# A spectral filter with a mixture of experts: batch 0's last routing, the splitting of expert weights and batch 1's crossing product are rearranged

## The chip, the cores and the metric

The kernel runs on one core of a Trainium2 chip. The metric is device microseconds of one execution. An execution of the kernel before takes 1332.23 us (median of three runs, 1332.09 to 1335.22). PE is the matmul engine (TensorE), PEld its weight loads, DVE the vector engine, ACT the scalar engine, POOL the GpSimd engine, and SP the engine that here only issues transfers (DMA).

## The reference, cut to what matters

```python
X = np.fft.rfft(x, axis=1)                       # x: (8, 2496, 256)
y = np.fft.irfft(X * (filt_r + 1j * filt_i)[None], n=2496, axis=1)
x = y.reshape(8 * 2496, 256)
xn = x / (norm(x) + 1e-06); en = emb / (norm(emb) + 1e-06)      # 8 experts
logits = xn @ en.T / tau
expert = argmax(logits); gate = softmax(logits)[expert]
out[rows of e] = gate * (maximum(rows @ w1[e], 0) @ w2[e])      # 256 -> 1024 -> 256
```

All in f32. Every row goes to one expert, so 19,968 rows are sorted by expert on the chip.

## The kernel before, in words

The transform. 2496 = 64 x 39, so the transform of a batch is a product over 39 (`s1`), a product over 64 (`s2`), the filter, a product back over 64 (`sa`, constant `m1`), and a product back over 39 (`sb`, `csb`). Between them data changes its layout: batch 0 does it on the chip (`conv_first`), later batches through DRAM, `SD` after `s1` and `ZD` after `sa`. Real and imaginary parts stand in 64 partitions each. The filter multiplies both by the real part of the filter (`yy`) and the crossed parts by its imaginary part (`xs`); for the crossing, two ACT copies exchange the halves of 64 partitions (L673, L674), and an addition brings `yy` and `xs` together (L681) before `sa`.

The routing. `conv_sb` works through 11 pairs of tiles. For each it makes the rows (f16 high and low part, `rows`), transposes them (`tp`, `yT`) and multiplies with the expert vectors (`lp`). In chunks of 3, 4 and 4 pairs `route` then finds the largest logit, its one-hot (`oh`), the running count by products with triangles (`rk`), the row's position in the sorted buffer `XS` (`ixi`), the exponentials (`ex`) and the gate (`se`, written into each row). Rows are sent by POOL, 128 at a time (`scatter_rows`). In batch 0 the factor `f` of a chunk comes from 12 steps of a root and two products on POOL (L169 to L178, L794, L795).

The experts. A slot is 256 rows of one expert. SP reads them transposed (`xT`), `up` makes `ph` in four parts of 12 products, ACT and DVE make the rectified high and low part (`h`), `down` adds 12 products into `po` two parts later. Weights are held as f16 pairs. `weight_halves` makes them for one expert after the other, one step at each call of `next(prep)`: the largest magnitudes (DVE for `w1`, ACT for `w2`: `wj`), a product with the identity and one with ones to spread the largest over partitions (`pm`, `ps`; `spread_max`), scales (`wsc`), and then four quarters `j` (`halves`): the high part on ACT, the low part on DVE. The first quarter of experts 1 to 7 is scaled and rounded by two ACT passes instead, and its low part is a POOL subtraction (L319 to L321).

What sets the order. Until the routing of batch 0 is done, the order on PE, DVE, ACT and SP is that in which the code is written; two tables, `WLOADS` and `PREPS`, say at which step of `head` an expert's weights are loaded and a step of `weight_halves` is made. After it, slots of batch g and the transform of batch g+1 are mixed: `spread` is called twice for each part of a slot, makes one step of `weight_halves`, every fourth time a load, and as many steps of the next batch as `pace` asks for. A planner of the framework then fixes each engine's queue. Every engine works its queue in order, so an instruction that waits holds all behind it.

Of the kernel before, what the change touches and what calls it, by code (L numbers as in the profile page):

```python
# [53 lines left out]
WLOADS = (0, 13, 17, 19, 26, 28, 36, 38, 44, 48)  # L54
PREPS = (21, 25, 57, 58, 59, 60, 66, 67, 68, 69, 70, 71, 72, 73)
# [4 lines left out]
def moe_spectral_kernel(  # L60
# [8 lines left out]
    m1: bass.AP,  # L69
    csb: bass.AP,  # L70
# [45 lines left out]
    csb_sb = const.tile([120, P], F32, tag="csb", name="csb_sb")  # L116
    sgn_sb = const.tile([P, NK2], F32, tag="sgn", name="sgn_sb")
# [3 lines left out]
    for q, t, a in ((nc.scalar, c1_sb, c1), (nc.scalar, c2_sb, c2), (nc.gpsimd, sgn_sb, sgn), (nc.gpsimd, m1_sb, m1),  # L121
                    (nc.gpsimd, emb_sb, emb), (nc.gpsimd, lt32, lt), (nc.gpsimd, tau_sb, tau),
                    (nc.gpsimd, csb_sb, csb)):
        q.dma_start(t, a)
# [24 lines left out]
    snoi = cst.tile([1, smax], I32, tag="st", name="snoi")  # L149
    nc.gpsimd.iota(snoi, pattern=[[1, smax]], base=0, channel_multiplier=0)  # L150
    sno = const.tile([1, smax], F32, tag="sno", name="sno")
# [69 lines left out]
    wmax = const.tile([P, E, 2], F32, tag="wmax", name="wmax")  # L221
    one32 = const.tile([2, P], F32, tag="one32", name="one32")
    nc.vector.memset(one32, 1.0)
    wtop = const.tile([2, E], F32, tag="wtop", name="wtop")
    wdg = const.tile([2, E, 2], F32, tag="wdg", name="wdg")
# [40 lines left out]
    def weight_halves():  # L266
# [3 lines left out]
        def largest(e, j):  # L270
            pieces = raws[e, j][0] + raws[e, j][1]
            wm = wmx[:, j * 4:j * 4 + len(pieces)]
            for i, r in enumerate(pieces):
                if j:
                    wjunk = cw.tile([P, 1024], F16, tag="hl", bufs=XYB, name=f"wj{e}_{i}")
                    with behind("relu"):
                        nc.scalar.activation(wjunk[:, :r.shape[1]], r, AF.Abs, accum_out=wm[:, i:i + 1])
                else:
                    with behind("lower"):
                        v.tensor_reduce(out=wm[:, i:i + 1], in_=r, axis=AX.X, op=ALU.max, apply_absolute_value=True)  # L280
            v.tensor_reduce(out=wmax[:, e, j:j + 1], in_=wm, axis=AX.X, op=ALU.add if j else ALU.max)

        def spread_max(e, js):

            n = js.stop - js.start
            m = wmax[:, e, js]
            v.tensor_scalar(out=m, in0=m, scalar1=2.0 ** -100, scalar2=None, op0=ALU.max)
            v.tensor_scalar(out=m.bitcast(I32), in0=m.bitcast(I32), scalar1=0x7F800000, scalar2=None,
                            op0=ALU.bitwise_and)
            yield  # L290
# [7 lines left out]
            nc.tensor.matmul(pm[:, :n], one32[:n], wdg[:n, e, :n], start=True, stop=True)  # L298
            v.tensor_scalar(out=wsc[:, e, js].bitcast(I32), in0=pm[:, :n].bitcast(I32), scalar1=0x7F800000,
                            scalar2=None, op0=ALU.bitwise_xor)  # L300

        def scales(e, js):
            for j in range(js.start, js.stop):
                v.tensor_scalar(out=wsc[:, e, j:j + 1], in0=wsc[:, e, j:j + 1], scalar1=2.0 ** (14 if j else 5),
                                scalar2=None, op0=ALU.mult)
            v.reciprocal(winv[:, e, js], wsc[:, e, js])
            if js.stop == 2:
                v.tensor_tensor(out=isc[:, e:e + 1], in0=winv[:, e, 0:1], in1=winv[:, e, 1:2], op=ALU.mult)
# [1043 lines left out]
```

## Time and profile before

| what | us |
|---|---|
| median of the runs | 1332.23 |
| profiled execution | 1332.51 |
| its span, first to last instruction | 1330.7 |
| PE busy | 1252.1 (94%) |
| DVE busy | 889.9 (67%) |
| ACT busy | 745.5 (56%) |
| POOL busy | 550.0 (41%) |
| mean granted TensorE clock, full speed 1 | 0.969 |

A busy share is a mean over stages. The rows below are from single stages: the first expert product begins at 123.29 us, the first product of `y` of batch 1 at 216.36, the first expert product of batch 1 at 303.37. In a row `L106 PE MATMUL ph<-xT,W` is line, engine, operation, and what is written from what; `x24` is a count; what stands in brackets is the idle time of the engine just before, and what ended it.

### The profile page before, as it was taken

The numbers are of one execution on the slowest core, as the hardware profiler recorded it, in microseconds if no ns is written. First come the engines' busy times: TensorE is split into PE (matmuls) and PEld (weight loads), VectorE is DVE, ScalarE is ACT, GpSimd is POOL, SyncE is SP. The second block draws the span as 40 slices with busy tenths as digits, with TensorE's granted clock in tenths as the row PEclk, the third lists the DMA queues.
The fourth block names the chain that finished last, engine by engine and source line by source line (L and its number), as shares of the span: only waits on it lengthen the run. The fifth ranks groups of instructions, "written<-read, shape, count | busy, mean of one in ns | idle before, by whom it ended". The sixth has DMA issues, their size and how long they took to land.

```text
span 1330.7 us, 32603 instructions
## 1 busy us (share of the span) xinstructions
PE 1252.1 (94%) x11240; PEld 1001.9 (75%) x11240; DVE 889.9 (67%) x2853; ACT 745.5 (56%) x1694; POOL 550.0 (41%) x642
## 2 busy tenths in 40 slices
PE   8866889989998999999999999999999999999997
PEld 6533556656677877777787778778878888999997
DVE  3564977875576768858775968597669622466664
ACT  5745577745645665658476747675666233333332
POOL 2363344474354525642654374346423632222222
PEclk9877899979999999999999999999999999999999
DMA  9728856678768775877697678766752422222221
GB/s 327 264 65 247 270 139 172 171 217 229 192 170 209 212 189 153 256 202 185 173 230 213 168 184 240 187 179 183 218 152 58 115 75 49 53 46 49 50 47 37
DMA packets 223223, 218.70 MB, mean 164 GB/s; under 512 B 125006, under 2 KB 168429, under 8 KB 221132
## 3 DMA queue, kind: packets, MB, share of 16 engines
q1 hardware_dynamic: 197226, 158.68, 44.8%
q0 software_dynamic: 25552, 57.72, 14.2%
q8 instruction: 94, 1.54, 0.5%
q14 instruction: 77, 0.63, 0.2%
q10 hardware_dynamic: 274, 0.13, 0.0%
HBM read 116.37 MB, written 79.60 MB: 147 GB/s over the span
## 4 chain that ended last, share of the span: by engine, by line
PE 57%; issue 13%; DVE 8%; DMA 8%; ACT 6%; POOL 5%; SPq 1%; POOLq 0%; ACTq 0%; DVEq 0%
PE ph L1106 20%; PE po L1134 18%; PE s L476 6%; POOL out_dram L1038 3%; PE y L481 3%; PE tp L809 3%; DMA f<-ZD 2%; PE sa L481 2%; DMA a<-SD 2%; PE s L481 2%; PE y L476 1%; DMA f<-in_filt 1%; PE lp L824 1%; PE sa L699 1%; DVE xs L647 1%
## 5 line engine op out<-in xcount | busy, mean ns | idle before, releaser
L1134 PE MATMUL po<-W,h 128*128 128x256 f16 (+1 forms) x3864 | 499.7, 274 | 3.4 <-ACT h L1112 2.1
L1134 PEld LDWEIGHTS <-h 128*128 128x128 f16 x3864 | 367.8, 98 | 89.2 <-issue 45.1
L1106 PE MATMUL ph<-xT,W 128*128 128x256 f16 x3072 | 400.9, 276 | 13.7 <-DVE h L1113 6.4
L1106 PEld LDWEIGHTS <-W 128*128 128x128 f16 x3072 | 295.9, 99 | 93.1 <-issue 45.9
L1112 ACT ACTIVATE h<-ph 128x512 f16<-128x512 f32 (+1 forms) x388 | 203.7, 526 | 259.4 <-PE ph L1106 198.9
L1113 DVE SCALAR_TENSOR_TENSOR h<-ph,h 128x512 f16<-128x512 f32 (+1 forms) x388 | 231.1, 596 | 140.4 <-ACT h L1112 139.1
L1038 POOL DMA_INDIRECT out_dram<-o,meta x161 | 177.5, 1103 | 324.3 <-ACT o L1141 284.9
L938 POOL DMA_INDIRECT XS<-rows,ixi x176 | 178.8, 1016 | 96.8 <-issue 66.5
L436 POOL DMA_DIRECT2D in<-in_x x72 | 57.0, 793 | 166.9 <-PE s L476 138.7
L681 POOL TENSOR_TENSOR yy<-yy,xs 128x512 f32<-128x512 f32 x56 | 75.0, 1339 | 99.9 <-DVE xs L647 62.6
L1106 PE MATMUL ph<-xT,wp 128*128 128x128 f16 x1584 | 104.8, 219 | 0.0
L1106 PEld LDWEIGHTS <-wp 128*128 128x128 f16 x1584 | 96.7, 98 | 2.5 <-issue 0.2
L476 PE MATMUL s<-in,c_sb 117*128 117x512 f32 (+1 forms) x168 | 91.2, 636 | 6.9 <-DMA in<-in_x 4.4
L1092 DVE COPY wp<-W 128x1024 f16 x132 | 58.1, 441 | 50.0 <-PE ph L1106 49.5
L758 DVE SCALAR_TENSOR_TENSOR rows<-y,rr,rows 128x256 f16<-128x256 f32 x176 | 76.6, 476 | 14.1 <-ACT rows L755 12.5
L755 ACT ACTIVATE rows<-y,rr 128x256 f16<-128x256 f32 x176 | 73.9, 479 | 18.7 <-DVE rr L788 16.2
L645 DVE TENSOR_TENSOR yy<-s,f 128x256 f32<-128x256 f32 x140 | 53.2, 417 | 45.1 <-ACT xs L674 34.3
L1141 ACT ACTIVATE o<-po,meta 128x256 f32<-128x256 f32 x161 | 69.7, 476 | 23.4 <-PE po L1134 18.9
L783 ACT ACTIVATE rows<-y 128x256 f16<-128x256 f32 x176 | 66.4, 387 | 16.8 <-PE y L476 10.3
L507 ACT COPY s<-s 128x512 f32<-128x512 f32 x77 | 45.2, 589 | 54.1 <-PE s L476 52.9
L809 PE MATMUL tp<-ident,rows 128*128 128x128 f16 x704 | 62.6, 223 | 6.9 <-DVE tot L915 4.8
L449 ACT CAST yp<-yy 128x512 fp32r<-128x512 f32 x50 | 30.9, 618 | 66.5 <-POOL yy L681 60.1
(233 smaller groups left out, 1675.5 us busy)
## 6 DMA issues: line engine op xcount, KB each, us to landing
f<-in_filt SPq DMA_DIRECT2D x148, 256.0 KB
a<-SD SPq DMA_DIRECT2D x70, 256.0 KB
ZD<-z SPq DMA_DIRECT2D x70, 256.0 KB
SD<-s SPq DMA_DIRECT2D x70, 240.0 KB
f<-ZD SPq DMA_DIRECT2D x70, 240.0 KB
W<-in_w SPq DMA_DIRECT2D x15, 1024.0 KB
in<-in_x POOLq DMA_DIRECT2D x60, 234.0 KB
in<-in_x SPq DMA_DIRECT2D x20, 234.0 KB
```

The costliest lines, as they stand in the source:

```text
L476: nc.tensor.matmul(out_, c[:a.shape[0]], a, start=True, stop=True)
L481: nc.tensor.matmul(out_, w[:k], b, start=(n == 0), stop=(n == 2))
L681: (nc.vector if k < 2 else nc.gpsimd).tensor_tensor(out=yy, in0=yy, in1=xs, op=ALU.add)
L755: nc.scalar.activation(rows[:, i, 0:D], y[:, i], AF.Copy, scale=rr[:, u:u + 1])
L758: nc.vector.scalar_tensor_tensor(out=rows[:, i, D:2 * D], in0=y[:, i], scalar=rr[:, u:u + 1], in1=rows[:, i, 0:D], op0=ALU.mult, op1=ALU.s ...
L809: nc.tensor.transpose(tp[:, i, j], rows[:, i, j * P:(j + 1) * P], ident)
L938: i = nc.gpsimd.indirect_dma_start(out=XS, out_offset=bass.IndirectOffsetOnAxis(ap=ix, axis=0), in_=src, in_offset=None)
L1038: i = nc.gpsimd.indirect_dma_start(out=out, out_offset=bass.IndirectOffsetOnAxis(ap=idx, axis=0), in_=o, in_offset=None, bounds_check=NT - ...
L1106: last["pe"] = nc.tensor.matmul(ph[:, fi, :size], wp[:, k * 2 + wh, fi * P:(fi + 1) * P], xT[:, xh * 2 + k], start=(c == 0), stop=(c == 5))
L1112: last["relu"] = nc.scalar.activation(h[:, 0, :, :size], ph[:, :, :size], AF.Relu)
L1113: hd = nc.vector.scalar_tensor_tensor(out=h[:, 1, :, :size], in0=ph[:, :, :size], scalar=0.0, in1=h[:, 0, :, :size], op0=ALU.max, op1=ALU. ...
L1134: nc.tensor.matmul(self.po[:, s], self.hs[fp][:, hh, fi, s * P:(s + 1) * P], self.Wp[:, off + wh * 1024:off + wh * 1024 + D], start=(fp == ...
```

## The change

- Crossing of batch 1 (`conv_s2` with g = 1): no copies and no addition. `xs` is made from the uncrossed product, and a second product with a constant `mx` (the halves of `m1` exchanged, sign turned) is added to `sa` in PE's accumulator.
- Scales: the largest magnitudes of the four quarters go through one product of four columns; clamping, the power of two and the turn of the exponent are put into steps that are there anyway.
- Quarters: the first quarter is split like the others (ACT, DVE); for experts 1 to 7 the last one is multiplied by the scale on POOL, rounded by ACT, subtracted on POOL. Expert 0's high parts are all made before its low parts.
- `PREPS` has 26 steps instead of 14, `WLOADS` two more loads; later loads come at every fourth call, three calls later.
- Routing of batch 0: the factor `f` of the last chunk is made on DVE; in the other chunks `f` is used only after the positions. One step of the gate is fused into the next.
- `s1` of batch 1: its stores are issued by ACT, one tile later, and three of its evacuations are DVE's. The last two additions of batch 0's filter are DVE's.
- The block numbers `sno` are held for one piece and shifted for each.

```diff
-WLOADS = (0, 13, 17, 19, 26, 28, 36, 38, 44, 48)
-PREPS = (21, 25, 57, 58, 59, 60, 66, 67, 68, 69, 70, 71, 72, 73)
+WLOADS = (0, 13, 17, 19, 26, 28, 36, 38, 44, 48, 60, 61)
+PREPS = (21, 25, 46, 48, 51, 53, 58, 58, 59, 60, 63, 63, 63, 63, 64, 64, 66, 67, 67, 68, 68, 69, 70, 70, 72, 73)
...
+        def spread_max(e, js, n):
+
+            k = js.stop - js.start
             pm = ps_c.tile([P, P], F32, tag="c", name=f"pm{e}_{js.start}")
-            nc.tensor.matmul(pm[:n], m, ident32, start=True, stop=True)
+            nc.tensor.matmul(pm[:n], wmx[:, :n], ident32, start=True, stop=True)
             v.tensor_reduce(out=wtop[:n, e:e + 1], in_=pm[:n], axis=AX.X, op=ALU.max)
-            v.tensor_scalar(out=wdg[:n, e, :n], in0=ident32[:n, :n], scalar1=wtop[:n, e:e + 1], scalar2=None,
-                            op0=ALU.mult)
+            if k == 2:
+                v.tensor_scalar(out=wdg[:n, e], in0=w2x[:n], scalar1=wtop[:n, e:e + 1], scalar2=2.0 ** -100,
+                                op0=ALU.mult, op1=ALU.max)
...
+        def halves(e, j, hi_too=True, lo_too=True):
...
-                if j == 0 and e:
-                    with behind("relu"):
-                        nc.scalar.activation(raw, raw, AF.Copy, scale=sc)
-                    nc.scalar.copy(hi, raw)
-                    nc.gpsimd.tensor_tensor(out=lo, in0=raw, in1=hi, op=ALU.subtract)
-                else:
+                aside = e and j == 3
+                if hi_too:
+                    if aside:
+                        nc.gpsimd.tensor_scalar(out=raw, in0=raw, scalar1=sc, scalar2=None, op0=ALU.mult)
                     with behind("relu"):
-                        nc.scalar.activation(hi, raw, AF.Copy, scale=sc)
-                    v.scalar_tensor_tensor(out=lo, in0=raw, scalar=sc, in1=hi, op0=ALU.mult, op1=ALU.subtract)
+                        nc.scalar.activation(hi, raw, AF.Copy, scale=1.0 if aside else sc)
+                if lo_too:
+                    if aside:
+                        nc.gpsimd.tensor_tensor(out=lo, in0=raw, in1=hi, op=ALU.subtract)
+                    else:
+                        v.scalar_tensor_tensor(out=lo, in0=raw, scalar=sc, in1=hi, op0=ALU.mult, op1=ALU.subtract)
...
-            nc.scalar.copy(st, pt)
-            for h, k, m in whole(g, buf_at(g, SD[g]), t, freqs, 120):
-                nc.sync.dma_start(m, st[:k, h])
+            if g == 1 and t > 5 and t % 2 == 0:
+                nc.vector.tensor_copy(st, pt)
+            else:
+                nc.scalar.copy(st, pt)
+            outs.append([(m, st[:k, h]) for h, k, m in whole(g, buf_at(g, SD[g]), t, freqs, 120)])
+            while len(outs) > (1 if g == 1 and t + 1 < NTL else 0):
+                for m, a in outs.pop(0):
+                    (nc.scalar if g == 1 else nc.sync).dma_start(m, a)
...
-                nc.scalar.copy(xs[0:NA], pt[NA:P])
-                nc.scalar.copy(xs[NA:P], pt[0:NA])
+                if g > 1:
+                    nc.scalar.copy(xs[0:NA], pt[NA:P])
+                    nc.scalar.copy(xs[NA:P], pt[0:NA])
...
-                filtered(xs, xs, fts, 1)
+                filtered(xs, xs if g > 1 else pt, fts, 1)
                 ys[k] = [yy]
-                if g:
+                if g > 1:
                     (nc.vector if k < 2 else nc.gpsimd).tensor_tensor(out=yy, in0=yy, in1=xs, op=ALU.add)
...
-                        nc.tensor.matmul(zp, cons["m1"], t.rearrange("p j c -> p (j c)"), start=(n == 0),
+                        nc.tensor.matmul(zp, mx_sb if n else cons["m1"], t.rearrange("p j c -> p (j c)"), start=(n == 0),
...
+            if g == 0 and s == NTL + 1:
+                gates(nc.vector)
...
+        late = g == 0 and not part_
+        if late:
+            yield 1
         else:
-            v.reciprocal(f, f)
-            v.tensor_tensor(out=d, in0=d, in1=bc(f), op=ALU.mult)
-            yield 1
-        ex = big("ex")
-        nc.scalar.activation(ex, d, AF.Exp)
-        if g:
-            yield 1
+            gates()
+            if g:
+                yield 1
...
-        if run["n"] % 4 == 0:
+        if run["n"] % 4 == 3:
             next(loads, None)
```

How the order changes, at three places. On DVE, the routing of batch 0's last chunk; `wtop`, `wdg` and `wsc` belong to the scale of expert 0, `l`, `d`, `ws` to the chunk. Before:

```order
L340 TENSOR_REDUCE wmax<-wmx 128x1
L287 TENSOR_SCALAR wmax<-wmax 128x2
L288 TENSOR_SCALAR wmax<-wmax 128x2
L293 TENSOR_REDUCE wtop<-pm_0_1204 2x1
L294 TENSOR_SCALAR wdg<-ident_138,wtop 2x2
L811 COPY yT_10_1217<-tp_10_1208 128x1024
L299 TENSOR_SCALAR wsc<-ps_0_1227 128x2
L865 TENSOR_REDUCE l_7_1245<-lp_7_1150 128x64
L867 TENSOR_REDUCE mx_7_1248<-l_7_1245 128x8
L869 TENSOR_TENSOR d_7_1246<-l_7_1245,mx_7_1248 128x64
L871 SCALAR_TENSOR_TENSOR ws_7_1247<-d_7_1246,w_146 128x64
```

And now, where `n`, `sg` and `f` are the factor of the chunk:

```order
L176 SCALAR_TENSOR_TENSOR n_10_1108<-sg_10_1107 128x8
L177 TENSOR_TENSOR n_10_1108<-n_10_1108,ssq_7_963 128x8
L178 SCALAR_TENSOR_TENSOR sg_10_1107<-n_10_1108,sg_10_1107 128x8
L179 TENSOR_TENSOR sg_10_1107<-sg_10_1107,ssq_7_963 128x8
L180 TENSOR_SCALAR sg_10_1107<-sg_10_1107 128x8
L805 TENSOR_TENSOR sg_10_1107<-sg_10_1107,rr_7_964 128x8
L806 TENSOR_SCALAR f_10_1109<-sg_10_1107,tau_169 128x8
L827 COPY yT_10_1220<-tp_10_1211 128x1024
L881 TENSOR_REDUCE l_7_1247<-lp_7_1146 128x64
L883 TENSOR_REDUCE mx_7_1250<-l_7_1247 128x8
L885 TENSOR_TENSOR d_7_1248<-l_7_1247,mx_7_1250 128x64
L887 SCALAR_TENSOR_TENSOR ws_7_1249<-d_7_1248,w_148 128x64
```

The scale of expert 0 is gone from ahead of the chunk (it now stands beside tiles 6 and 7), and the steps that POOL made are there instead.

On POOL, the rows of batch 0's last chunks and what follows. `XS` is the sorted buffer, `W` the weights. Before:

```order
L178 TENSOR_SCALAR sg_10_1093<-sg_10_1093 128x8
L794 TENSOR_TENSOR sg_10_1093<-sg_10_1093,rr_7_956 128x8
L795 TENSOR_SCALAR f_10_1095<-sg_10_1093,tau_167 128x8
L938 DMA XS<-rows_7_957,ixi_7_1288 178304x258 x2
L938 DMA XS<-rows_8_996,ixi_7_1288 178304x258 x2
L938 DMA XS<-rows_9_1036,ixi_7_1288 178304x258 x2
L938 DMA XS<-rows_10_1084,ixi_7_1288 178304x258 x2
L799 IOTA rows_0_2074 128x2
L321 TENSOR_TENSOR W<-W 128x1024
L1038 DMA out_dram<-o_0_0_1782,meta_0_1403 19968x256
```

And now:

```order
L962 DMA XS<-rows_6_865,ixi_3_1128 178304x258 x2
L962 DMA XS<-rows_7_965,ixi_7_1283 178304x258 x2
L962 DMA XS<-rows_8_1004,ixi_7_1283 178304x258 x2
L962 DMA XS<-rows_9_1048,ixi_7_1283 178304x258 x2
L962 DMA XS<-rows_10_1098,ixi_7_1283 178304x258 x2
L322 TENSOR_SCALAR W<-W,wsc 128x1024
L327 TENSOR_TENSOR W<-W 128x1024
L813 IOTA rows_0_2024 128x2
L322 TENSOR_SCALAR W<-W,wsc 128x1024
L327 TENSOR_TENSOR W<-W 128x1024
L1063 DMA out_dram<-o_0_0_1747,meta_0_1419 19968x256
```

The steps between the rows of two chunks are gone; two passes over a quarter of expert 1 follow at once, and two of expert 2 before the first results leave.

On SP, what stands before the first read of sorted rows (`xT`). Before:

```order
L436 DMA in_10_1348<-in_x 117x256
L436 DMA in_10_1348<-in_x 39x256
L509 DMA SD_179<-s_7_1355 120x2x256
L509 DMA SD_179<-s_8_1362 120x2x256
L509 DMA SD_179<-s_9_1370 120x2x256
L509 DMA SD_179<-s_10_1383 120x256
L509 DMA SD_179<-s_10_1383 40x256
L1073 DMA_TRANSPOSE xT_0_1401<-XS 128x4x256
L1075 DMA meta_0_1403<-XS 128x2x2
L1073 DMA_TRANSPOSE xT_1_1405<-XS 128x4x256
```

And now:

```order
L439 DMA in_8_1339<-in_x 117x2x256
L439 DMA in_9_1350<-in_x 117x2x256
L439 DMA in_10_1362<-in_x 117x256
L439 DMA in_10_1362<-in_x 39x256
L1098 DMA_TRANSPOSE xT_0_1417<-XS 128x4x256
L1100 DMA meta_0_1419<-XS 128x2x2
L1098 DMA_TRANSPOSE xT_1_1421<-XS 128x4x256
L1100 DMA meta_1_1423<-XS 128x2x2
L643 DMA f_0_1444<-in_filt 128x512
L643 DMA f_1_1446<-in_filt 128x512
```

The stores of `s` are gone from SP's queue. They stand on ACT, mixed with evacuations and expert passes ahead of the first `h`:

```order
L514 COPY s_7_1371<-s_1_7_1369 128x512
L518 DMA SD_185<-s_6_1359 120x2x256
L324 ACTIVATE W<-W 128x1024
L518 DMA SD_185<-s_7_1371 120x2x256
L284 ACTIVATE wj_0_1386,wmx<-W 128x1024
L284 ACTIVATE wj_1_1388,wmx<-W 128x1024
L514 COPY s_9_1392<-s_1_9_1390 128x512
L518 DMA SD_185<-s_8_1381 120x2x256
L518 DMA SD_185<-s_9_1392 120x2x256
L518 DMA SD_185<-s_10_1398 120x256
L518 DMA SD_185<-s_10_1398 40x256
L1137 ACTIVATE h_0_0_1438<-ph_0_0_1425 128x512
```

## Rows read from the trace of the kernel before

**Rows 1.** Busy time by stage: each engine, TensorE's clock, DMA share, GB/s.

```profile
core 0: us, PE busy (x) PEld busy (x) DVE busy (x) ACT busy (x) POOL busy (x), PEclk, DMA share, GB/s
123.20:216.30 93.10, 82.14 (x522) 56.23 (x523) 71.07 (x143) 64.95 (x101) 32.97 (x26) 0.89 0.71 209
216.30:303.30 87.00, 77.52 (x577) 51.31 (x576) 69.02 (x261) 54.63 (x130) 45.23 (x51) 0.90 0.70 190
303.30:344.40 41.10, 41.03 (x281) 29.09 (x280) 18.14 (x43) 21.51 (x41) 19.00 (x18) 1.00 0.85 225
```

**Rows 2.** The critical chain, 303.3 to 310 us: start, us, what.

```profile
305.28 0.86 PE s L476 x2
...
307.98 1.31 PE ph L1106 x12
```

**Rows 3.** PE's groups, 123.2 to 216.3 us: count, busy, mean, idle before.

```profile
L1106 PE MATMUL ph<-xT,W 128*128 128x256 f16 x240 | 34.1, 296 | 5.6 <-DMA xT<-XS 2.3 <-ACT W L320 2.0 <-DVE h L1113 1.0
L1134 PE MATMUL po<-W,h 128*128 128x256 f16 x223 | 29.1, 273 | 2.6 <-ACT h L1112 2.1 <-DVE h L1113 0.4
L476 PE MATMUL s<-a,c_sb 128*128 128x512 f32 x20 | 12.5, 713 | 1.6 <-ACT z L702 1.6
L699 PE MATMUL sa<-yy,m_sb 128*128 128x512 f32 x20 | 12.1, 691 | 0.3 <-DVE yy L645 0.3
```

**Rows 4.** PE in order of time, 92 to 124 us.

```profile
92.64 3.76 PE L476 MATMUL s<-in,c_sb 117*128 117x512 f32 x4
...
123.29 1.04 PE L1106 MATMUL ph<-xT,W 128*128 128x256 f16 x4 [2.27 <-DMA xT<-XS]
```

**Rows 5.** DVE in order of time, 83 to 102 us.

```profile
83.27 0.20 DVE L892 RECIPROCAL f<-f 128x8 f32<-128x8 f32 x1 [2.44 <-POOL f L795]
...
94.69 0.22 DVE L885 TENSOR_TENSOR oh<-w,mv 128x64 f16<-128x64 f32 x1
...
100.53 0.20 DVE L892 RECIPROCAL f<-f 128x8 f32<-128x8 f32 x1 [5.61 <-POOL f L795]
...
101.88 0.17 DVE L918 CAST ixi<-ix 128x8 int32<-128x8 f32 x1
```

**Rows 6.** POOL in order of time, 97 to 114 us.

```profile
97.97 0.98 POOL L938 DMA_INDIRECT XS<-rows,ixi  x1 [0.30 <-issue]
...
103.08 1.07 POOL L938 DMA_INDIRECT XS<-rows,ixi  x1 [2.59 <-DVE wsc L304]
...
113.80 0.90 POOL L938 DMA_INDIRECT XS<-rows,ixi  x1 [0.30 <-issue]
```

**Rows 7.** SP's queue in order of time, 111 to 120 us.

```profile
111.74 8.04 SPq L509 DMA_DIRECT2D SD<-s  x5
119.87 1.35 SPq L1073 DMA_TRANSPOSE xT<-XS  x1
```

**Rows 8.** ACT's groups, 123.2 to 216.3 us.

```profile
L277 ACT ACTIVATE wj<-W 128x1024 f16<-128x1024 f32 x10 | 10.5, 1050 | 0.1
...
L673 ACT COPY xs<-s 64x512 f32<-64x512 f32 x10 | 5.8, 582 | 8.0 <-PE s L476 7.9
...
L319 ACT ACTIVATE W<-W,wsc 128x1024 f32<-128x1024 f32 x5 | 5.7, 1146 | 2.6 <-DVE wsc L304 2.5
```

**Rows 9.** POOL: one group of 123.2 to 216.3 us, one pass in time.

```profile
L681 POOL TENSOR_TENSOR yy<-yy,xs 128x512 f32<-128x512 f32 x8 | 10.2, 1270 | 11.6 <-DVE wmax L281 6.1 <-DVE xs L647 5.4
...
219.78 2.13 POOL L321 TENSOR_TENSOR W<-W 128x1024 f16<-128x1024 f32 x1
```

**Rows 10.** ACT's queue at the start.

```profile
0.73 1.04 ACTq L124 DMA_DIRECT2D c_sb<-in_c  x2
```

**Rows 11.** DVE and POOL in order of time, 151.8 to 152.5 us.

```profile
151.91 1.27 DVE L287 TENSOR_SCALAR wmax<-wmax 128x2 f32<-128x2 f32 x1
...
151.90 1.26 POOL L681 TENSOR_TENSOR yy<-yy,xs 128x512 f32<-128x512 f32 x1 [5.30 <-DVE wmax L281]
```

More of the change, by code (lines that the diff above doesn't have):

```diff
@@ L283, in spread_max @@
[L283 to L290, printed above, removed]
+                        v.tensor_reduce(out=m, in_=r, axis=AX.X, op=ALU.max, apply_absolute_value=True)
+                yield
+        def spread_max(e, js, n):
+            k = js.stop - js.start
@@ L310, in halves, with scales @@
-        def halves(e, j):
+            nc.tensor.matmul(pm[:, :k], one32[:n], wdg[:n, e, :k], start=True, stop=True)
+            v.tensor_scalar(out=wsc[:, e, js].bitcast(I32), in0=pm[:, :k].bitcast(I32), scalar1=0x7F800000,
+                            scalar2=0x7F800000, op0=ALU.bitwise_and, op1=ALU.bitwise_xor)
+        def scales(e):
+            v.reciprocal(winv[:, e], wsc[:, e])
+            v.tensor_tensor(out=isc[:, e:e + 1], in0=winv[:, e, 0:1], in1=winv[:, e, 1:2], op=ALU.mult)
+        def halves(e, j, hi_too=True, lo_too=True):
@@ L329, in maxima @@
                 next(loads)
[L330 to L348 removed]
+            for j in range(2):
+                for _ in largest(e, j, 2 * j):
+                    if e == 0:
+                        yield
+                if e:
+                    yield
+            yield from spread_max(e, slice(0, 2), 4)
+            yield
         for e in range(E - 1):
@@ L353, in weight_halves @@
                     yield from maxima(n)
-            scales(e, slice(0, 2))
             for j in range(4):
-                halves(e, j)
+                halves(e, j, lo_too=e > 0)
+                if e == 0:
+                    yield
+                    continue
                 if j == 3:
+                    scales(e)
                     prepped[0] = e + 1
                 yield
+            if e == 0:
+                for j in range(4):
+                    halves(e, j, hi_too=False)
+                    yield
+                scales(e)
+                prepped[0] = 1
         e = E - 1
@@ L365, in weight_halves @@
             yield
-            largest(e, j)
-            yield from spread_max(e, slice(j, j + 1))
+            for _ in largest(e, j, 0):
+                pass
+            yield from spread_max(e, slice(j, j + 1), 3 if j else 2)
             yield
-            scales(e, slice(j, j + 1))
             for k in order:
@@ L588, in conv_first @@
                 ys[k] = yy
-                nc.gpsimd.tensor_tensor(out=yy, in0=yy, in1=xs, op=ALU.add)
+                (nc.vector if k + 2 >= NK else nc.gpsimd).tensor_tensor(out=yy, in0=yy, in1=xs, op=ALU.add)
             yield W_S2
@@ L994, in block_table @@
             mk = tmp[:, 0:n * (E + 1)].rearrange("p (s e) -> p s e", e=E + 1)
-            s1 = sno[:, at:at + n]
+            s1 = sl.tile([1, PIECE], F32, tag="sn", name=f"sn{at}")[:, :n]
+            v.tensor_scalar(out=s1, in0=sno[:, :n], scalar1=float(at), scalar2=None, op0=ALU.add)
             v.memset(mk[:, :, 0:1], 1.0)
@@ L1333 @@
         "m1": m1,
+        "mx": mx,
         "csb": csb,
```

92 lines of the change are left out of this document (43 added, 49 removed).

## The prediction

> **What bounds the kernel now.** I read the stages first [rows 1]. The reader should see two kinds of time there. From 303.3 to 344.4 us PE is busy for 41.03 of 41.10 us at a granted clock of 1.00: a batch's transform and expert products run together, and nothing holds PE. From 123.2 to 216.3 us, where experts are also split into f16 halves, PE is busy for 82.14 of 93.10 us at 0.89, and the true slack is larger, as a count shows. The critical chain gives unit prices at full clock [rows 2]: 12 expert products in 1.31 us (0.109 each) and one f32 product of 512 columns in 0.86 (two instructions of 0.43). The stage has 240 + 223 expert products, 50.5 us, and 40 f32 instructions of `s` and `sa`, 17.2 us [rows 3]: 67.7 us of work in 93.1, so 25.4 of slack. Some 2 us of it are small products that I don't count. This slack, and what lies before the first expert product, is what a change in this place can win. After 344 us the same instructions stand in nearly the same order, and I put nothing there.
>
> Then I read how the first expert product comes to start at 123.29 us [rows 4]. DVE has the one-hot of batch 0's last chunk at 94.91, but the next instruction of its queue waits until 100.53 for `f`, a chain of small steps on POOL, and the rows' positions are behind it (`ixi`, 102.05) [rows 5]. POOL sends rows of the chunk before until 98.95, with the chain behind them, then idles 2.59 us before it may send the last chunk: 103.08 to 114.70 [rows 6]. SP issues the transposed read `xT` only at 119.87, behind stores of `s` that hold its queue from 111.74 [rows 7].
>
> **The change part by part.** The sum is made against the profiled execution: span 1330.7 us, 1332.5 with what lies around it; the median of the runs is 1332.23, so the same number serves.
>
> *Last chunk of batch 0.* Its `f` moves to DVE as 13 more steps, and POOL has none. From 100.53 to 101.88 DVE made six steps, 0.225 us each, so 13 cost 2.9 us ahead of the one-hot. Against that the wait of 2.44 us at 83.27 goes [rows 5], since the `f` of that chunk now stands behind its positions. Expert 0's magnitude passes (1.05 each [rows 8]) move up on ACT, and the first chunk's exponential waits behind its positions with the next tile's evacuation queued behind it; but the two PE trips of expert 0's scale go out of the last chunk's way. I let these cancel: one-hot at about 95. Two `s` products stood between it and the positions on PE, 3.76 us for four instructions [rows 4]. One stays in front, so positions come at about 96.7 and row weights at 97.7. Then POOL decides: it ends the previous chunk at about 98.5, and eight scatters take the 11.6 us of rows 6, or 10.4 if none is slowed: done at 109.5, not 114.7.
>
> *Two experts split while rows leave.* The second halves of expert 0 and the splitting of expert 1 fall here, and in PE's queue the scale of expert 2 now stands ahead of the first expert product. Behind the scatters POOL multiplies the last quarter of expert 1, an operation that the trace doesn't have. Nearest rows [rows 9]: two-input passes, 1.27 us for 512 columns and 2.13 for 1024. I take 2.13, for its size. ACT waits for it in its queue and copies (1.15), takes two magnitude passes of expert 2 (2.1); PE, DVE and PE make the scale (two tiny products with DVE steps of 0.2 between; an estimate of 1.8): 109.5 + 2.1 + 1.15 + 2.1 + 1.8 = 116.7. DVE has second halves and maxima to make beside two POOL passes; I add 1.3 for that: **first expert product at 118, 5.3 us earlier**. The read of xT isn't what ends last then: from its issue to the product were 3.4 us, SP has no stores in front, and if it is issued 2 us after the last scatter (5.2 now), it is there at 115. That is the lower bound, -8.5. The upper is 0: twelve stores are issued by ACT, and an ACT issue took 0.52 us at the program's start [rows 10], 6.2 us in a queue that has 18 us of work from 87 us on (eight halves, four magnitude passes, eight copies); it would still be done by 112, if waits don't add up.
>
> The Trainium skill (GPSIMD Engine Reference, section Engine selection) says that a one-input elementwise pass on GpSimd runs at roughly line rate. An estimate from that page's clock of 1.2 GHz is 0.9 us for 1024 columns, and the sum would come out 1.2 us lower; no run here shows it.
>
> *Crossing by a second product.* Batch 1 has ten steps. Each loses two ACT copies of 64 partitions (20 x 0.58 = 11.6 us [rows 8]) and an addition, eight of them on POOL (10.2 us [rows 9]). PE gets ten f32 products: 20 x 0.43 = **+8.6 us of work**, to 76.3.
>
> *Splitting of experts 1 to 7.* A quarter that took two ACT passes (the first 1.146 [rows 8]) and a POOL pass now takes one ACT and one DVE pass; another quarter goes from DVE to two POOL passes. ACT loses about 1.1 for each expert, DVE nothing, POOL gains one pass. In this stage ACT sheds 11.6 + 4.4 of its 64.95 busy us [rows 1], and one expert of those split there is done beforehand. Two expert loads move ahead of the stage too.
>
> *How much slack is left?* Ends: the 2 us of small work, as clean as 303 to 344, or all 25.4. The idle that PE shows there [rows 3] is for expert weights from ACT (2.0), for `h` from ACT (2.1), for `z` from ACT (1.6): ACT's relief bears on all three. I take 11, nearer the clean stage: 76.3 + 11 = 87.3 against 93.1, **-5.8**. Ends: -14.8 and +8.6.
>
> *216 to 303.* The order is nearly the same; one POOL pass now stands between scatters of batch 1 (up to +2.1), and a second half moves off DVE. I take 0, with -3 to +3. The smaller edits (one DVE step more in each piece of the block table, two additions of batch 0 from POOL to DVE, a fused step, loads three calls later) lie beside PE work or replace as much; at nothing, with 1.3 us either way, one POOL addition.
>
> Sum: 1332.5 - 5.3 - 5.8 = **1321.4**.
>
> **The rivals.**
> *The stage becomes clean.* PE runs 123 to 216 as it does 303 to 344, and the start is bound by xT: -8.5 - 14.8, so 1309.2. For it: ACT is named behind most of PE's waits, and loses a quarter of its work. Against: two scale products for each expert still block PE's queue until DVE and ACT have its maxima.
>
> *Given back before 303.* Batch 1's first expert product starts at 303.3, where I cut the stage, and needs that batch's whole route. If DVE sets this route (69.02 busy of 87.00 us, rows 1), the gain turns into PE idle there: about 1332. For it: PE had 9.5 idle us in that stage. Against: each link of the route starts from PE work that comes earlier too.
>
> *POOL holds DVE.* At 151.90 POOL starts an addition of 1.26 us; a DVE step over two columns starts at 151.91 and takes 1.27 [rows 11]. So a POOL pass can keep even a tiny DVE step until it ends. POOL loses eight passes of 1.27 (10.2) and gains up to seven of 2.13 (14.9), 4.7 us more of holding. If DVE paces the experts, and not ACT, the slack grows by that and the second products lie open on PE: -5.3 + 8.6 + 4.7, so 1340.5. It decides from the point where DVE's scale steps or second halves end later than PE needs them, which is if slack stays above 20. The Trainium skill (SBUF — State Buffer, section SBUF: two separate sides) has it as a rule: DVE and GpSimd share one port pair, locked for a whole instruction, and the loser blocks fully. By that rule each added POOL pass is such a lock; the trace agrees with 1.27 us at 151.91.
>
> **How the numbers follow.** Forecast 0.48 (own range 1315 to 1328), clean stage 0.22, given back 0.17, POOL holds DVE 0.13. Within 0.3% is 4 us, about what a measurement of this kernel can tell from no change. Faster: 0.48 + 0.22 + a quarter of 0.17, about 0.74. Slower: most of 0.13 and a little of the third, 0.12. Same: 0.14. The range reaches beyond the clean case (1307) and the given-back one (1336), leaving out some 2 in 10.
>
> **What would show it.** Right: the last chunk's first scatter at 98 to 100 us with no idle on POOL before it, the first expert product at 116 to 120; up to the first `y` product of batch 1 no PE wait for a W tile, a clock of 0.95 or more, a stage of 85 to 91 us. The start is wrong if ACT's queue with its stores ends after 117, or the scale of expert 2 holds PE beyond 120. The stage is wrong if DVE steps of 0.2 us take 1 to 2 beside POOL's W passes while PE waits. The whole is wrong if batch 1's first expert product stays near 303.

## The result, and the profile after

The changed kernel takes 1320.25 us (median of six runs, 1314.41 to 1326.20) against 1332.16 (six runs, 1328.64 to 1335.22). The ratio is 0.9913, with a 95% interval of 0.9886 to 0.994. The forecast was 1321.4. Timed once more in the experiments below it took 1317.90, ratio 0.9907 (0.9879 to 0.9936). So it is faster by 0.6 to 1.2%, and the forecast's direction and size both stand. Its terms do not stand as well as its sum.

I cut the trace after where I cut the one before. The columns are those of [rows 1]; the first row ends at batch 1's first `y` product, the second at its first expert product.

```profile
116.30:196.60 80.30, 80.30 (x529) 56.29 (x528) 54.89 (x103) 40.78 (x66) 28.11 (x18) 0.97 0.73 212
196.60:287.30 90.70, 80.37 (x590) 51.55 (x591) 70.66 (x255) 56.13 (x133) 55.16 (x56) 0.91 0.75 203
```

The reader should see that PE's busy time equals the length of the first row: nothing holds it, where it had lost 10.96 of 93.10 us before, and the clock is 0.97 instead of 0.89. ACT fell from 64.95 to 40.78 us and DVE from 71.07 to 54.89. The second row is longer than before (87.00). What stands in the first stage, against [rows 3]:

```profile
L1131 PE MATMUL ph<-xT,W 128*128 128x256 f16 x240 | 32.5, 285 | 0.0
L1159 PE MATMUL po<-W,h 128*128 128x256 f16 x216 | 27.8, 273 | 0.0
L479 PE MATMUL s<-a,c_sb 128*128 128x512 f32 x20 | 10.4, 604 | 0.0
...
L708 PE MATMUL sa<-xs,mx_sb 128*128 128x512 f32 x20 | 10.2, 592 | 0.0
L304 PE MATMUL ps<-wdg,one 4*128 4x2 f32 x7 | 1.5, 270 | 0.0
L294 PE MATMUL pm<-ident,wmx 128*4 128x128 f32 x6 | 1.1, 273 | 0.0
```

The new products cost 10.2 us, and `s` has fallen from 12.5 to 10.4 for the same 20 instructions. Before, four of them ran between 157 and 168 us, where the granted clock had fallen to the lower of its two levels, 1.2 of 2.4 GHz (0.58 from 156 to 160 us, 0.50 to 168), after PE had been busy for 3.7 of 6 us; the slowest took 1222 ns. Now none takes more than 697. The two kinds of products of the scale, `pm` and `ps`, for which PE's queue waited 3.1 us before, find their inputs ready. Before, they were:

```profile
L298 PE MATMUL ps<-wdg,one 2*128 2x2 f32 x8 | 1.7, 282 | 1.8 <-DVE wdg L294 1.8
L292 PE MATMUL pm<-ident,wmax 128*2 128x128 f32 x8 | 1.5, 271 | 1.3 <-DVE wmax L288 1.3
```

How the first expert product comes to start, first on POOL (start, duration, what; in brackets the idle time before):

```profile
92.91 1.39 POOL L962 DMA_INDIRECT XS<-rows,ixi  x1 [0.76 <-ACT s L514]
...
103.45 0.90 POOL L962 DMA_INDIRECT XS<-rows,ixi  x1 [0.30 <-issue]
104.40 2.86 POOL L322 TENSOR_SCALAR W<-W,wsc 128x1024 f32<-128x1024 f32 x1
108.74 2.83 POOL L327 TENSOR_TENSOR W<-W 128x1024 f16<-128x1024 f32 x1 [1.48 <-DMA in<-in_x]
```

then on DVE:

```profile
109.69 1.89 DVE L310 TENSOR_TENSOR isc<-winv 128x1 f32<-128x1 f32 x1
...
112.11 2.33 DVE L287 TENSOR_REDUCE wmx<-W 128x1 f32<-128x1024 f32 x2
```

on SP:

```profile
108.59 1.38 SPq L1098 DMA_TRANSPOSE xT<-XS  x1
```

and on PE:

```profile
114.58 0.58 PE L294 MATMUL pm<-ident,wmx 128*4 128x128 f32 x2 [1.02 <-DVE wmx L287]
115.79 0.58 PE L304 MATMUL ps<-wdg,one 4*128 4x2 f32 x2 [0.62 <-DVE wdg L297]
116.31 4.87 PE L1131 MATMUL ph<-xT,W 128*128 128x256 f16 x24
```

The last chunk's first scatter moved from 103.08 [rows 6] to 92.91, and the read of `xT` from 119.87 [rows 7] to 108.59. The rows are not what the first expert product waits for any more: the scale of expert 2 is. Its magnitudes stand on DVE behind a step over one column, which took 1.89 us because it began beside POOL's subtraction of 108.74 to 111.57 (quarter1dve below takes that pass away).

The span is PE's busy time and its idle time. This table has both for all kernels that ran, from the traced execution, with that execution's own time, the median, and the ratio of the runs to those of the kernel before that were timed beside them (its medians lie from 1331.42 to 1333.10). A traced execution can lie away from its median: that of oldroute is the slowest of twelve.

| kernel | PE busy | PE idle | traced | median | ratio (95%) |
|---|---|---|---|---|---|
| before | 1252.1 | 78.6 | 1332.51 | 1332.16 | 1 |
| changed | 1249.0 | 63.6 | 1314.41 | 1320.25 | 0.9913 (0.9886 to 0.994) |
| changed, again | 1254.8 | 59.0 | 1315.64 | 1317.90 | 0.9907 (0.9879 to 0.9936) |
| nocross | 1244.0 | 70.5 | 1316.28 | 1316.11 | 0.9882 (0.9852 to 0.9913) |
| oldroute | 1254.3 | 77.1 | 1333.24 | 1325.39 | 0.995 (0.9931 to 0.9968) |
| noscale2 | 1249.2 | 68.5 | 1319.61 | 1319.27 | 0.9906 (0.988 to 0.9932) |
| oldprep | 1248.7 | 71.2 | 1321.70 | 1319.12 | 0.9896 (0.9873 to 0.9919) |
| dvequarter | 1246.7 | 66.0 | 1314.44 | 1318.41 | 0.9897 (0.9876 to 0.9919) |
| quarter1dve | 1246.9 | 66.1 | 1314.83 | 1315.82 | 0.9879 (0.9855 to 0.9902) |
| spstores | 1249.4 | 62.7 | 1313.91 | 1318.17 | 0.9894 (0.9871 to 0.9918) |
| neither | 1245.7 | 76.9 | 1324.45 | 1322.50 | 0.9931 (0.9911 to 0.9952) |
| onlycross | 1247.7 | 77.2 | 1326.66 | 1328.06 | 0.9979 (0.996 to 0.9999) |
| onlyroute | 1246.7 | 91.3 | 1339.87 | 1340.61 | 1.0088 (1.0057 to 1.0119) |
| nocross_q1 | 1241.3 | 67.2 | 1310.31 | 1313.35 | 0.988 (0.9851 to 0.9909) |

### The profile page after: what moved, and what is told of

Its sections match the earlier page's. It is cut to its first block, busy times and chain, and to the rows that moved or that the text cites. A ratio compares the mean times of both kernels' runs of the same rounds, so it can differ in the third digit from the quotient of the medians.

```text
span 1312.6 us, 32545 instructions
## 1 busy us (share of the span) xinstructions
PE 1249.0 (95%) x11260; PEld 999.0 (76%) x11260; DVE 883.9 (67%) x2800; ACT 725.2 (55%) x1664; POOL 554.0 (42%) x624
## 5 line engine op out<-in xcount | busy, mean ns | idle before, releaser
L691 POOL TENSOR_TENSOR yy<-yy,xs 128x512 f32<-128x512 f32 x48 | 66.3, 1380 | 88.4 <-DVE xs L656 52.3
L1117 DVE COPY wp<-W 128x1024 f16 x132 | 61.1, 464 | 49.9 <-PE ph L1131 49.3
L792 ACT ACTIVATE rows<-y 128x256 f16<-128x256 f32 x176 | 66.4, 387 | 20.6 <-PE y L479 13.5
```

Of the source, the lines that this page charges most:

```text
L691: (nc.vector if k < 2 else nc.gpsimd).tensor_tensor(out=yy, in0=yy, in1=xs, op=ALU.add)
L792: nc.scalar.activation(rows[:, i, D:2 * D], y[:, i], AF.Square, accum_out=ssq[:, u + i:u + i + 1])
```

## The experiments

**The changed kernel again.** No edit.

> The changed kernel itself, timed again. Its six runs lay between 1314.4 and 1326.2 us, and the traced one is the fastest of them. If the trace at hand is typical, a second one shows the first expert product near 116.3 us, the stage to batch 1's first y product near 80.3, batch 1's first expert product near 287.3, and the median stays at 1316 to 1322. If the first trace was a lucky one, the stage is longer (84 to 88, as the prediction had it) or the granted clock after it is lower, with the same busy work.

The stage repeats (80.94 us, no idle), the start does not:

```profile
120.46:201.40 80.94, 80.94 (x530) 56.61 (x529) 55.03 (x103) 40.87 (x66) 27.94 (x18) 0.97 0.73 211
201.40:292.40 91.00, 80.34 (x590) 51.57 (x590) 70.74 (x255) 56.10 (x133) 55.33 (x56) 0.91 0.73 206
```

The first expert product came at 120.46 and batch 1's first at 292.40, both 4 to 5 us later than in the first trace. From 20 to 60 us the granted clock was 0.87 in this execution and 1.00 in the first trace; before, it was 0.87 as well. Against a trace of the same clock the start is won by 2.8 us, not 7.0. The other way round, onlycross (below) has the head of the kernel before, but for one more constant and the shorter block numbers, at a clock of 1.00, and its first expert product came at 120.84; against that the first trace wins 4.5. Each of the two traced executions is the fastest of its six runs.

**Crossing as before.** In `conv_s2`:

```diff
-                if g > 1:
+                if g:
                     nc.scalar.copy(xs[0:NA], pt[NA:P])
                     nc.scalar.copy(xs[NA:P], pt[0:NA])
...
-                filtered(xs, xs if g > 1 else pt, fts, 1)
+                filtered(xs, xs if g else pt, fts, 1)
...
-                if g > 1:
+                if g:
                     (nc.vector if k < 2 else nc.gpsimd).tensor_tensor(out=yy, in0=yy, in1=xs, op=ALU.add)
```

> The changed kernel with batch 1's crossing as it was: two copies of 64 partitions on ACT and an addition in each of ten steps, no second product. Theory A (the copies and additions are what made PE wait there): PE sheds 10.2 us of products in this stage, but the idle comes back, so the stage stays at 80 or goes up to 85 and the time is the changed kernel's or up to 5 us more. Theory B (expert 1 and the scale of expert 2 being made ahead is what emptied the stage of waits): the stage falls towards 72, and the time is 5 to 8 us less than the changed kernel's.

```profile
117.81:198.61 80.80, 76.49 (x524) 54.59 (x523) 63.78 (x109) 53.92 (x88) 40.25 (x27) 0.96 0.72 212
```

The stage is as long as with the second products, and 4.3 us of idle came back, 3.6 of it ended by DVE's `h` and `yy`. In it PE also made 13 more expert products and two more of `s` than the changed kernel, 2.3 us of work at the prices of [rows 2]. Theory A holds for the stage, but the time did not rise: 1316.11, an interval that overlaps the changed kernel's. The crossing costs 5 to 11 us of busy time and saves 7 to 12 of idle time (the table): in this kernel it is worth nothing that I can measure.

**Routing as before.**

```diff
-                    if t + 1 < NTL:
-                        gates(nc.gpsimd)
+                    gates(nc.gpsimd)
...
-            if g == 0 and s == NTL + 1:
-                gates(nc.vector)
...
-        late = g == 0 and not part_
-        if late:
-            yield 1
-        else:
-            gates()
-            if g:
-                yield 1
+        gates()
+        yield 1
...
-        if late:
-            gates()
+        if g == 0:
             yield 1
```

> The changed kernel with the routing of batch 0 as it was: the factor of the last chunk on POOL, used ahead of the positions in every chunk. Theory A (the start of the experts is set by the rows' route): first scatter of the last chunk back from 93 to about 100 us, first expert product from 116.3 to 120 to 123, and the time 4 to 7 us more than the changed kernel's. Theory B (the scale of expert 2 ahead of it in PE's queue sets the start): scatters later, but the first expert product within 2 us of 116.3 and the time within 2 us.

The time is Theory A's: 1325.39, 5 to 7 us above the changed kernel, with intervals that overlap by less than 0.001. The first expert product came later than it said, at 132.27; but this trace is the slowest of twelve runs, and had a clock of 0.87 from 20 to 60 us, so it belongs beside the 120.46 of the second trace. POOL had `f` at 102.58, but the last chunk's row weights stood in DVE's queue behind expert 0's low halves and expert 1's magnitudes, which the new table puts there:

```profile
102.26 0.32 POOL L806 TENSOR_SCALAR f<-sg,tau 128x8 f32<-128x8 f32 x1
112.27 1.07 POOL L953 DMA_INDIRECT XS<-rows,ixi  x1 [9.69 <-DVE rows L940]
```

So part of the loss is that the table and the routing were made for each other, and this run does not price the routing alone.

**Without the scale of expert 2 in the head.** The last four entries of `PREPS` (70, 70, 72, 73) are left out.

> The changed kernel without the last four steps of the head's table: expert 1 is still split ahead, but the largest magnitudes and the scale of expert 2 are made after the first expert products. Theory A (in the changed kernel the rows have long been there, since the read of xT is issued at 108.6 us, and the scale of expert 2 with a DVE step held by a POOL pass keeps PE until 116.3): the first expert product comes at 112 to 114, and if the stage stays without waits the time is 2 to 4 us less than the changed kernel's. Theory B (the scale is work that has to be done anyway, and done later it makes PE wait for expert 2's weights): the first product comes earlier, but the stage grows by as much or more, and the time is the same or up to 4 us longer.

```profile
113.87 2.79 PE L1131 MATMUL ph<-xT,W 128*128 128x256 f16 x24 [0.64 <-DMA xT<-XS]
...
141.59 1.52 PE L708 MATMUL sa<-yy,m_sb 128*128 128x512 f32 x2 [3.48 <-DVE xs L656]
```

The start is bound by `xT`, at 113.87, as Theory A said; the stage grew to 86.14 with 5.1 of idle, as Theory B said, and 1319.27 is Theory B's time. Its reason isn't what the trace shows: PE did not wait for expert 2's weights but 3.5 us for DVE's `xs`, and DVE had waited for a tile of the filter from DRAM. The earlier start is no gain here.

**Expert 1 not split ahead.** `PREPS` keeps its first 18 entries (to 67).

> The changed kernel with only the first 18 steps of the head's table: expert 0 is split and expert 1's scale made before the first expert product, as in the kernel before; expert 1's quarters and expert 2's scale come later. Four fewer steps gave a start 2.5 us earlier, and a stage 5 to 6 us longer (86.1 after 80.3 and 80.9). Theory A (an expert split ahead is what empties the stage of waits): the first expert product comes at 113 to 115, as early as the read of xT allows, the stage grows further to 89 to 93, and the time is 2 to 5 us above the changed kernel's 1318 to 1320. Theory B (the crossing's copies were the load that mattered, so the relieved ACT and POOL take the splitting without a wait): the stage stays near 86, and the time is the changed kernel's or less.

First expert product at 113.93; the stage 85.04, idle 7.6, with 36 expert products fewer in it (3.9 us at [rows 2]) than in the changed kernel. So the stage is worse, as Theory A said, but 5.0 of the idle us are one wait, for batch 1's data on their way back from DRAM. PE got there at 120.34 us; the changed kernel's first trace began the same product at 126.22, without a wait:

```profile
125.31 3.63 PE L479 MATMUL s<-a,c_sb 128*128 128x512 f32 x4 [4.97 <-DMA a<-SD]
```

The time, 1319.12, is Theory B's: with the crossing by products, splitting expert 1 ahead is worth nothing that the medians show.

**No quarter on POOL, and expert 1's alone not on POOL.**

```diff
-                aside = e and j == 3
+                aside = False
```

> The changed kernel with every quarter split by ACT and DVE, none by POOL: it takes two POOL passes of 2.8 us from each of experts 1 to 6 and gives DVE a low half of 1.2 us for each. Theory A (POOL's passes hold DVE: in the changed kernel a DVE step over one column that starts beside such a pass takes 1.89 us where 0.16 is usual): without them the start comes 2 to 3 us earlier, the stage stays at 80 or 81 since DVE was busy for 55 of its 80 us, and the time falls by 2 to 4 us. Theory B (POOL takes work that would hold DVE or ACT just as long): the start moves by less than 1 us, the stage grows by up to 5, and the time is the same or up to 4 us longer.

The start moved by 0.4 us (115.91, at a clock of 0.96 from 20 to 60 us where the first trace had 1.00), and the time is 1318.41: Theory B. Its stage did not grow: 75.35 us without idle, with 36 expert products fewer in it. POOL's 37 us less busy time is neither a gain nor a loss. In the second version only expert 1 is excepted:

```diff
-                aside = e and j == 3
+                aside = e > 1 and j == 3
```

> The changed kernel with the last quarter of expert 1 alone split by ACT and DVE; those of experts 2 to 7 stay with POOL. Theory A (in the head the two POOL passes lie on the path to the first expert product: ACT waits for the first, and the second holds a DVE step ahead of expert 2's magnitudes): the first expert product comes 2 to 3 us earlier than in the changed kernel at the same clock in the head (about 114 where that has 116.3, or 118 where it has 120.5), the stage stays at 80 to 82, and the time falls by 1.5 to 3 us. Theory B (the quarter's DVE half of 1.2 us takes the place of the wait): the start moves by less than 1 us, and so does the time.

DVE, at the place where the changed kernel had 1.89 us:

```profile
110.04 0.16 DVE L310 TENSOR_TENSOR isc<-winv 128x1 f32<-128x1 f32 x1
...
110.75 2.33 DVE L287 TENSOR_REDUCE wmx<-W 128x1 f32<-128x1024 f32 x2
```

With no POOL pass beside it the same step takes 0.16 us, and the first expert product comes at 114.69, 1.6 earlier at the same clock (1.00 from 20 to 60 us). The time, 1315.82, is 2 to 4 us below the changed kernel's two medians, as Theory A said, but the intervals overlap: likely, not shown.

**Stores on SP.**

```diff
-                    (nc.scalar if g == 1 else nc.sync).dma_start(m, a)
+                    nc.sync.dma_start(m, a)
```

> The changed kernel with the stores of batch 1's first transform stage issued by SP again, and no other change. Theory A (the read of xT is behind them in SP's queue, as in the kernel before): the read goes out after the last store, at 115 to 117 us and not at 108.6, the first expert product comes at 119 to 121 where the changed kernel has 116.3, and the time is 2 to 5 us more. Theory B (the scale of expert 2 holds PE until 116.3 anyway, and an ACT queue without 12 issues brings that forward): the first product comes at 115 to 117 and the time stays within 1.5 us.

SP's queue:

```profile
107.64 8.54 SPq L518 DMA_DIRECT2D SD<-s  x6
116.27 1.35 SPq L1098 DMA_TRANSPOSE xT<-XS  x1
```

Theory A's mechanism is there: `xT` goes out at 116.27 and the first expert product at 119.58. Theory B's time is there: 1318.17. Three microseconds at the start did not reach the end.

**Crossing and splitting ahead both taken back.** The edits of the second and fifth experiment together.

> The changed kernel with both taken back: batch 1 crosses by copies and additions, and expert 1 is not split ahead. Each taken back alone left the time where it was (1316 and 1319 beside 1318 to 1320). Theory A (the two stand in for each other: either makes enough room on ACT, and only without both does PE wait as before): from the first expert product to batch 1's first takes 180 us or more, as in the kernel before (180.1), against 171.0 and 171.9 in the changed one, and the time is 1323 to 1328. Theory B (neither is worth anything; the gain is the route's, the quarters' and the loads'): the time stays at 1315 to 1320.

```profile
114.94:202.68 87.74, 78.48 (x523) 54.72 (x523) 66.81 (x112) 58.25 (x94) 41.91 (x28) 0.92 0.68 199
```

From the first expert product to batch 1's first (299.93) it took 185.0 us, where nocross took 173.3 and oldprep 178.0, and the idle and the lower clock are back. The median, 1322.50, is just below Theory A's range; its interval (0.9911 to 0.9952) lies above those of nocross (0.9852 to 0.9913) and oldprep (0.9873 to 0.9919) but for a touch, and overlaps both of the changed kernel's. I read it as Theory A: with one of the two the other adds nothing that the medians show. That is likely, not shown. That ACT's room is the reason is not shown either. Of the 9.3 idle us ACT ended 2.2, DVE 2.4, and one wait for data from DRAM, as in oldprep, 4.3:

```profile
124.94 3.78 PE L479 MATMUL s<-a,c_sb 128*128 128x512 f32 x4 [4.32 <-DMA a<-SD]
```

And 1322.50 is still 9 us below the kernel before timed beside it (1331.53). What the merged scale, the first quarter and the earlier loads make of these 9 was not tried.

**The crossing alone, in the kernel before.** The edits of `conv_s2` and the constant `mx`; the shorter block numbers come with it.

> The kernel before with the crossing alone (and the shorter block numbers, for room). Theory A (the copies' 11.6 us on ACT were what PE waited for): the stage falls from 93 to 86 us or less despite 8.6 us more of products, and the time is 4 to 8 us below the kernel before. Theory B (the scale of each expert and its weights are what PE waits for, and the products are paid in full where they don't fill a wait): the stage stays at 92 to 98, and the time is within 3 us of the kernel before, or above it.

```profile
120.84:209.93 89.09, 82.54 (x529) 56.29 (x529) 63.22 (x140) 52.59 (x80) 22.29 (x18) 0.98 0.70 219
```

The stage fell by 3.8 us with 10.2 us of second products in it (and 13 fewer of `po`); the time by 0.2% (0.996 to 0.9999). That lies between the theories.

**The routing alone, in the kernel before.** The opposite of the third experiment's edit.

> The kernel before with the routing edits alone (the last chunk's factor on DVE, positions ahead of the factor in the other chunks). Theory A (the route is the gain's larger half by itself): the last chunk's first scatter moves from 103 to about 95 to 97, the first expert product from 123.3 to 117 to 120, and the time is 4 to 7 us below the kernel before, as taking the route out of the changed kernel cost 7. Theory B (the start is next bound by SP's stores, which stand ahead of xT, and by expert 0's splitting, so the route pays only together with the table and the stores): the first expert product at 121 to 123, the time within 3 us of the kernel before.

This is slower than before, which neither theory had. The scatters end at 107.63, 7 us earlier, but SP issues `xT` only at 118.70, behind five stores. The first expert product comes at 121.93, at a clock of 0.92 from 20 to 60 us; with the start of before at 123.29 (0.87) and 120.84 (1.00, onlycross) that is no gain shown (Theory B). In the stage, three of DVE's filter products start just behind POOL's subtraction for an expert. One of them on DVE, the subtraction on POOL, then the stage's row and PE's first group in it:

```profile
164.68 2.35 DVE L647 SCALAR_TENSOR_TENSOR xs<-xs,sgn_sb,f 128x256 f32<-128x256 f32 x1
```

```profile
164.42 2.33 POOL L321 TENSOR_TENSOR W<-W 128x1024 f16<-128x1024 f32 x1 [7.69 <-ACT W L320]
```

```profile
121.93:223.52 101.59, 84.34 (x538) 57.71 (x539) 74.44 (x142) 63.54 (x99) 30.67 (x24) 0.90 0.62 191
```

```profile
L1122 PE MATMUL ph<-xT,W 128*128 128x256 f16 x240 | 32.4, 289 | 13.1 <-ACT W L320 7.4 <-DVE h L1129 2.5 <-DMA xT<-XS 2.3
```

The 20 filter products on DVE took 16.5 us instead of 9.4, ACT waited 7.9 us for DVE's `wsc` (2.5 before), and PE 7.4 us for ACT's weights. The three began within 0.3 us of a subtraction; before, the nearest began 1.9 to 3.7 us after one. That the collisions are the whole 8.7 us by which the stage grew (1.9 of it is 17 more `po` products) was not tried by itself.

**Best version.** The edits of nocross and quarter1dve together.

> Best version so far by the runs: the changed kernel with the crossing by copies, and with expert 1's last quarter split by ACT and DVE. Each alone read 1316 against the changed kernel's 1318 to 1320. If they add up: 1312 to 1315, first expert product 114 to 115 at full clock in the head. If ACT becomes short of time again with both (it has the copies back, and DVE one pass more): 1316 to 1319.

```profile
115.96:190.10 74.14, 73.74 (x520) 53.72 (x519) 57.38 (x104) 52.38 (x86) 38.78 (x27) 0.96 0.77 229
```

The median is 1313.35, the lowest of all, in the range for both gains adding up; PE's busy time is the lowest too. Its ratio, 0.988 (0.9851 to 0.9909), overlaps the changed kernel's, so it is faster than the kernel before, and only likely faster than the changed one.

## Why the prediction was right

By stretch, against the trace of before, in us:

| stretch | predicted | trace after | again |
|---|---|---|---|
| to the first expert product | -5.3 | -7.0 | -2.8 |
| to batch 1's first `y` | -5.8 | -12.6 | -12.0 |
| to batch 1's first expert product | 0 | +3.5 | +3.8 |
| from there to the end | 0 | -2.1 | -5.9 |
| span | -11.1 | -18.1 | -16.9 |

The medians fell by 11.9 and 13.5. The traced executions won more than the typical run; what the other runs lose, no trace shows (their mean granted clock was 0.968 to 0.974 where the first trace had 0.978). So that the sum, 1321.4, lies so near the medians is in part luck: in the traces, from which its terms were made, the change won 6 to 7 us more than the 11.1 forecast. (Before, the first `y` product of batch 1 came at 216.20, which the table uses, not at 216.36.)

*The start* was forecast at -5.3. It is -2.8 in the trace with the clock of before, and -7.0 in the other. I had POOL end the chunk before at 98.5 and start the last one at 98 to 100. That chunk, whose positions no longer stand behind `f`, was gone at 92.15, and the last one's first scatter came at 92.91 (96.23 and 96.98 in the second trace). Against that the chain behind the scatters, which I had as 8.5 us (109.5 to 118), took 12.0 in both traces (104.35 to 116.31 in the first). These are two errors of opposite sign, so the size is luck where it fits. On DVE I counted six steps from 100.53 to 101.88; there are seven, and the 13 new ones took 2.6 us, not 2.9. POOL's multiplication, priced at 2.13 between 1.27 and 2.13, took 2.86, outside my bounds; and DVE's step was held for 1.89. The Trainium skill's rule (GPSIMD Engine Reference, section Engine selection), by which I worked out an estimate of 0.9 us for that pass, does not fit: the measurement decides, at three times as much. Of my signs that the start is wrong, the second trace shows two: ACT's queue with its stores ended at 120.25 (115.82 in the first trace; the bound was 117), and the scale of expert 2 stood ahead of PE's first expert product until 120.46 (the bound was 120). That `xT` would not be what ends last was right: in noscale2 PE started 3.5 us after its issue, and 3.5 us from 108.59 make 112.1 (an estimate).

*The stage* is the term that was mis-sized. What it should show is there (no wait for a `W` tile, a clock of 0.97), but at 80.3 us, below the 85 to 91 forecast. I took 11 us of slack beside 76.3 of work; there were 4.0 (80.30 less 76.3), 2.6 of them the scale's products, with no idle at all. That is the clean-stage rival's claim, 78.3, not the forecast's 87.3. What I held against that rival, the two scale products that block PE's queue for each expert, did not happen: their waits of 3.1 us are gone. [rows 3] had waits behind ACT, and ACT lost 24 of its 65 us, where I had counted 16. Which of the edits emptied the stage stays open. With copies, or with expert 1 split in the stage, PE idled 4.3 or 7.6 us and the medians did not rise; without both it idled 9.3 and the median lay 2 to 6 above the others. But most of these waits ended with DVE or with data from DRAM, not with ACT.

*216 to 303* was taken as 0 within 3, and became longer by 3.5 to 3.8. This is not the given-back rival, by which the gain turns into idle time of PE: that went from 9.5 us to 10.3 and 10.7. The rest is busy time (77.5, then 80.4 and 80.3): work that now lies on this side of the cut, eight more instructions of batch 2's transform above all. `s` and `sa` from 216 us to batch 1's first expert product, before and after:

```profile
L476 PE MATMUL s<-a,c_sb 128*128 128x512 f32 x8 | 4.1, 615 | 1.9 <-DVE yy L645 1.9
L699 PE MATMUL sa<-yy,m_sb 128*128 128x512 f32 x4 | 2.9, 824 | 0.0
```

```profile
L479 PE MATMUL s<-a,c_sb 128*128 128x512 f32 x12 | 10.0, 949 | 7.4 <-DMA a<-SD 5.5 <-ACT z L711 1.4 <-DVE yy L654 0.5
L708 PE MATMUL sa<-yy,m_sb 128*128 128x512 f32 x8 | 5.6, 795 | 0.5 <-DVE yy L654 0.5
```

Behind the cut PE's busy time is 2.6 and 3.2 us less (1004.1 before, 1001.4 and 1000.8). New is where PE waits, before the transform of batch 2:

```profile
265.14 3.75 PE L479 MATMUL s<-a,c_sb 128*128 128x512 f32 x4 [5.47 <-DMA a<-SD]
```

The way through DRAM (`s` to `SD` to `a`) stands open here (5.85 us in the second trace); before, the longest wait between 245 and 304 us was 1.90.

*POOL holds DVE* had the right mechanism, within limits. The trace bears out the Trainium skill's rule (SBUF — State Buffer, section SBUF: two separate sides), which the page states for DVE steps with two inputs in SBUF or in a two-port mode, beside POOL's subtraction: 1.89 for 0.16 in the head, 2.35 for 0.47 in onlyroute. Beside POOL's multiplication the same step ended before that pass did, so there the measurement does not show a lock for a whole instruction. DVE, then POOL:

```profile
116.81 1.05 DVE L310 TENSOR_TENSOR isc<-winv 128x1 f32<-128x1 f32 x1
```

```profile
116.73 2.84 POOL L322 TENSOR_SCALAR W<-W,wsc 128x1024 f32<-128x1024 f32 x1 [5.08 <-issue]
```

The rival did not decide here: PE had no wait in the stage, and DVE's load there fell by 16 us. In onlyroute it probably did. That its 1340.61 is the rival's 1340.5 is chance: onlyroute has neither the second products nor the added POOL passes from which the rival's number was made.

## What to carry to other kernels

Several edits that bear on the same waits need not add up: take them back one at a time, and then together, before counting any as worth its cost, and look in each trace at what PE then waits for, which can be another thing than the edit relieved. Read the end of the program by PE's busy and idle time and not by one early start: starts between 113.9 and 119.6 us came with medians of 1318 to 1319. Before comparing a stretch between two kernels, count the instructions in it and compare the granted clock ahead of it. A shorter chain does not pay while the queue behind it (here SP's stores) is the next to end, and it can shift work into a collision.

## What was not expected of the hardware

A one-input pass of POOL over 128x1024 in f32 takes 2.84 to 2.88 us (seven of them), more than a two-input pass with f16 output (2.12 at best). Beside it a DVE step of 0.16 us took 1.05; beside the two-input pass it was held to the end of that pass, 1.89. The granted clock of the first 100 us differs between executions of one kernel: 0.87 and 1.00 from 20 to 60 us, and in these two executions the first expert product stood 4.2 us apart. From 45 to 50 us PE was busy for 3.17 us in the one and 3.18 in the other; from 50 to 55 the granted clock was 0.57 in the one, most of it at the lower level, and 1.00 in the other.
